# Converting the second block's weights piece by piece, every 0.8 units of matmul work

## The chip, the cores and the metric

The kernel runs on one core of a Trainium2 chip. The metric is the device time of one execution in microseconds. An execution uses TensorE for matmuls (PE, with its weight loads PEld), VectorE (DVE), ScalarE (ACT), GpSimd (POOL) and SyncE (SP), whose queue issues all of this kernel's DMAs in order.

## The reference

Three stages follow each other on 4 sequences of 576 tokens and 512 features. First an attention with 8 heads of 64: a windowed one over the three nearest neighbours on either side, plus one over tokens that are averaged by fours. Then two blocks with residuals:

```python
def _moe_ref(x, g_ln, w_ch1, w_ch2):                        # w_ch1 512 x 2048
    xn = (x - mean(x)) / np.sqrt(var(x) + 1e-06) * g_ln
    return x + np.maximum(xn @ w_ch1, 0.0) @ w_ch2
...
def _moe2_ref(x, w_tok1, w_tok2, w_ch1, w_ch2):             # w_ch1 512 x 1536
    h = np.maximum(x.transpose(0, 2, 1) @ w_tok1, 0.0) @ w_tok2
    u = x + h.transpose(0, 2, 1)
    return u + np.maximum(u @ w_ch1, 0.0) @ w_ch2
```

The inputs q, k and v are float32, all weights are float64.

## The kernel before

**Tiling.** The 2304 tokens are cut into 9 chunks of 256. A *unit* is 128 hidden columns of a block's first weight matrix with the same 128 rows of its second: 16 units for the first block, 12 for the second. For a chunk and a unit, `g1` (line 622) multiplies the chunk's turned activations with the first matrix (12 matmuls, 128x256, into an `h` tile). ACT applies the ReLU and DVE forms the remainder (lines 635, 636, tile `ht`). `g2` (line 641) multiplies that with the second matrix (6 matmuls, 128x512, into `acc` tiles). Products are made of two parts each, a high and a low one, in three passes: high x high, high x low, low x high. The sequence has 9 x 16 units of the first block and 9 x 12 of the second, 252 in all. Units 0 to 143 are the first block's, and unit 144 is the second block's first one. In the emission `g1` of a unit stands ahead of `g2` of the unit before it.

**Weights.** The weights are float64, so each has to be taken apart. A unit comes in two *pieces* of 512 KB: piece 0 is its first matrix, piece 1 its second. `load_unit` (DMA at line 190) brings a piece into a staging tile `st`; two of them exist in the part of the program that matters here. `convert_steps` (line 143) turns it into the high and low parts in five steps: three on DVE (lines 149, 154, 159, tile `cv`), one on ACT (line 164, the high part), one on DVE (line 167, the low part). `split_unit` pins the place of the first of them among the other pinned work. After the five steps of a piece, `w_split` (line 817) emits the load of the next one. The load's own wait is that the third step (line 159) has read the staging tile. The 12 units of the second block, once converted, stay in SBUF for all nine chunks.

**Beside it.** The token mixing of the second block needs, for each of the 4 sequences, five loads `xr` (lines 705 and 707), their split on ACT and POOL (lines 713, 714, tile `xs`), the matmuls of `tok1` (line 729, tile `k`), a ReLU (lines 738, 739) and, for each chunk, those of `tok2` (line 760, tile `g`). A chunk's activations are turned by DVE in 32x32 blocks (line 579, tile `xc`) and then by 32 small DMAs of 16 KB per chunk (line 586, tile `xt`). These, the weight pieces and the `xr` loads all go through SP's one queue.

**What sets the order.** `put(pos, f)` (line 775) hangs work on a position that is counted in units: at a whole number ahead of `g2` of that unit, at a half behind it. Behind that a scheduler with a model of the engines' times sets each engine's final order; pinned instructions keep theirs.

Of the kernel before, what the change touches and what calls it, by code (L numbers as in the profile page):

```python
# [91 lines left out]
def block_kernel(ctx: ExitStack, tc: tile.TileContext, qk, vw, vg, g_ln, wa, t1, t2, wb, band, out):  # L92
    nc = tc.nc
    UA = wa.shape[0]
    UB = wb.shape[0]
# [80 lines left out]
    NPC = 2 * DM // QW  # L176
# [598 lines left out]
    def put(pos, f, *args):  # L775
        u, half = divmod(int(2 * pos), 2)
        u = min(u, NSEQ - 1)
        (bg if half else mid)[u].append(lambda: f(*args))
# [32 lines left out]
    def w_load(n):  # L811
        while n and nl[0] < len(pieces) and nl[0] - nsp[0] < sp["n"]:
            load_unit(*pieces[nl[0]])
            nl[0] += 1
            n -= 1
# [128 lines left out]
    bw = base[NCH - 1]  # L944
    put(bw + 1, units_b)
    put(bw + 1, lambda: w_load(sp["n"]))
    for m in range(UB):
        put(bw + 3.5 + m, w_split, NPC)
    for c in range(NCH, 2 * NCH):
        put_prep2(c, base[c] - 1)  # L950
    put_tok(2, base[NCH + 2])
# [96 lines left out]
```

## Time and profile before

| | |
|---|---|
| median of 3 runs | 951.56 us (948.16 to 956.02) |
| profiled execution, its own time | 952.27 us |
| its span | 950.5 us |
| PE busy | 916.2 us, 96% |
| DVE busy | 447.9 us, 47% |
| ACT busy | 280.6 us, 30% |
| POOL busy | 147.5 us, 16% |
| loads of second-block weights | 24 of 512 KB |

Busy time is what the profiler saw an engine execute; matmuls overlap in the array, so their single durations (some 0.28 and 0.40 us) are longer than the distance at which they follow each other. A timeline row gives the start in us from the span's start, the time it covers, the engine, the line and the operation, and in brackets how long the engine was idle ahead of it and for whom it waited.

### The profile page before, as it was taken

Reading aid. Unit: us, or ns where it says so; the run is one execution under the profiler, and the core shown is the slowest. Engines: PE = TensorE matmul, PEld = TensorE weight load, DVE = VectorE, ACT = ScalarE, POOL = GpSimd, SP = SyncE. Lnnn points to the kernel's source line nnn. Section 1 sums busy time; section 2 is a strip of 40 time slices with the busy share of each in tenths; the row PEclk is TensorE's granted clock in tenths of the full one; section 3 lists DMA queues with packets and bytes.
Section 4 is the critical chain, followed back from the end, with each engine's and each line's share of the span. In section 5 each row is a group of like instructions: output and inputs, shape, how many; then the busy total and the mean of one; then the engine's idle time right before and its main releaser. Section 6 shows DMA issues by size and latency. Waiting matters only on the chain.

```text
span 950.5 us, 17304 instructions
## 1 busy us (share of the span) xinstructions
PE 916.2 (96%) x6702; PEld 801.0 (84%) x6702; DVE 447.9 (47%) x1044; ACT 280.6 (30%) x809; POOL 147.5 (16%) x176
## 2 busy tenths in 40 slices
PE   7879999899999999999999999999999999999998
PEld 5667878778888888888889988787888888999997
DVE  4785788794225252276312267896322322222211
ACT  5444344344443343323111122332112111111111
POOL 6443214213322221111010000111001000000000
PEclk9888999999999999999999999999999999999999
DMA  8653565534232132234212025663212211110100
GB/s 221 183 188 115 157 194 182 169 104 106 83 105 67 47 104 62 67 106 144 73 28 63 23 83 150 190 187 111 57 44 63 51 36 33 45 35 13 44 23 23
DMA packets 113121, 89.78 MB, mean 94 GB/s; under 512 B 73264, under 2 KB 91952, under 8 KB 113040
## 3 DMA queue, kind: packets, MB, share of 16 engines
q1 hardware_dynamic: 113040, 88.68, 32.7%
q8 instruction: 53, 0.87, 0.4%
q14 instruction: 28, 0.23, 0.1%
HBM read 66.62 MB, written 14.16 MB: 85 GB/s over the span
## 4 chain that ended last, share of the span: by engine, by line
PE 78%; DVE 8%; DMA 8%; SPq 2%; ACT 1%; issue 1%; POOL 1%; DVEq 0%; ACTq 0%
PE h L629 33%; PE acc L650 31%; DMA up_scr<-od 2%; DMA st<-in_wb_dram 2%; PE k L650 2%; PE k L729 2%; SPq L586 2%; DMA xr<-x_scr 2%; DVE cv L159 2%; PE g L760 2%; DVE cv L154 1%; PE g L282 1%; PE g L363 1%; PE g L318 1%; PE g L468 1%
## 5 line engine op out<-in xcount | busy, mean ns | idle before, releaser
L629 PEld LDWEIGHTS h<-xt,w 128*128 128x128 f32 x3024 | 395.5, 190 | 25.0 <-ACT w L164 1.9
L629 PE MATMUL h<-xt,w 128*128 128x256 f32 x3024 | 411.8, 284 | 1.6 <-ACT w L164 1.0
L650 PE MATMUL acc<-w,ht 128*128 128x512 f32 x1416 | 378.7, 399 | 8.1 <-ACT ht L635 3.6
L650 PEld LDWEIGHTS acc<-w,ht 128*128 128x128 f32 x1416 | 252.2, 189 | 61.5 <-ACT ht L635 5.7
L636 DVE SCALAR_TENSOR_TENSOR ht<-h,ht 128x256 fp32r<-128x256 f32 x252 | 105.8, 421 | 354.6 <-ACT ht L635 354.3
L635 ACT ACTIVATE ht<-h 128x256 fp32r<-128x256 f32 x252 | 96.4, 383 | 394.0 <-PE h L629 370.4
L714 POOL TENSOR_TENSOR xs<-xr,xs 128x512 fp32r<-128x512 f32 x20 | 26.6, 1330 | 292.4 <-ACT xs L713 292.4
L164 ACT ACTIVATE w<-cv 128x512 fp32r<-128x512 f32 x56 | 35.5, 635 | 70.7 <-DVE cv L159 70.5
L346 POOL TENSOR_TENSOR vg<-vg 72x256 f32<-72x256 f32 x39 | 32.8, 841 | 144.7 <-DMA vg<-in_vg_dram 143.5
L167 DVE TENSOR_TENSOR w<-cv,w 128x512 fp32r<-128x512 f32 x56 | 42.6, 764 | 6.4 <-ACT w L164 6.2
L159 DVE SCALAR_TENSOR_TENSOR cv<-st,cv 128x512 int32<-128x512 int32 (+4 forms) x63 | 42.8, 684 | 0.6
L154 DVE SCALAR_TENSOR_TENSOR cv<-st,cv 128x512 int32<-128x512 int32 (+4 forms) x63 | 42.4, 677 | 0.7
L515 POOL TENSOR_TENSOR x<-x,pt 128x256 f32<-128x256 f32 (+2 forms) x44 | 28.0, 649 | 80.2 <-DMA x<-up_scr 47.9
L729 PE MATMUL k<-xs,t1w 128*128 128x512 f32 (+1 forms) x120 | 33.5, 410 | 2.2 <-ACT xs L713 1.4
L760 PE MATMUL g<-r,t2w 128*128 128x512 f32 x120 | 34.0, 395 | 0.0
L593 ACT ACTIVATE xt<-xt 128x512 fp32r<-128x512 f32 x30 | 19.0, 632 | 50.0 <-DMA xt<-xc 49.9
L149 DVE TENSOR_SCALAR cv<-st 128x512 int32<-128x512 int32 (+4 forms) x63 | 25.8, 412 | 13.8 <-DMA st<-in_wb_dram 8.9
L594 DVE TENSOR_TENSOR xt<-xt 128x512 fp32r<-128x512 f32 x30 | 20.6, 686 | 23.6 <-ACT xt L593 23.5
L650 PE MATMUL k<-w,ht 128*128 128x512 f32 x96 | 27.6, 409 | 0.1
L729 PEld LDWEIGHTS k<-xs,t1w 128*128 128x128 f32 (+1 forms) x120 | 19.1, 188 | 7.2 <-ACT xs L713 2.1
L502 ACT ACTIVATE pt<-g,rz 128x64 f32<-128x64 f32 (+1 forms) x78 | 17.4, 322 | 23.2 <-DVE rz L492 21.8
L760 PEld LDWEIGHTS g<-r,t2w 128*128 128x128 f32 x120 | 20.9, 189 | 3.0
(160 smaller groups left out, 700.6 us busy)
## 6 DMA issues: line engine op xcount, KB each, us to landing
st<-in_wa_dram SPq DMA_DIRECT2D x28, 512.0 KB
st<-in_wb_dram SPq DMA_DIRECT2D x24, 512.0 KB
xt<-xc SPq DMA_DIRECT2D x480, 16.0 KB
qk<-in_qk_dram SPq DMA_DIRECT2D x13, 579.0 KB
x_scr<-x SPq DMA_DIRECT2D x18, 256.0 KB
x<-x_scr SPq DMA_DIRECT2D x9, 512.0 KB
out_dram<-x SPq DMA_DIRECT2D x18, 256.0 KB
vw<-in_vw_dram SPq DMA_DIRECT2D x13, 319.9 KB
```

Of the source, the lines that this page charges most:

```text
L154: nc.vector.scalar_tensor_tensor(out=f, in0=h, scalar=-0x40000000, in1=f, op0=ALU.bitwise_and, op1=ALU.bitwise_or)
L159: nc.vector.scalar_tensor_tensor(out=f, in0=l, scalar=29, in1=f, op0=ALU.logical_shift_right, op1=ALU.bitwise_or)
L164: nc.scalar.activation(out=hi, in_=f.bitcast(F32), func=ACTF.Copy)
L167: nc.vector.tensor_tensor(out=lo, in0=f.bitcast(F32), in1=f32(hi), op=ALU.subtract)
L346: nc.gpsimd.tensor_tensor(out=vd[:, :, :, :D], in0=vd[:, :, :, :D], in1=vgt[:, :, o:o + 128].rearrange("p c (h d) -> p c h d", h=2), op=AL ...
L515: (eng or nc.gpsimd).tensor_tensor(out=x, in0=x, in1=tmp[rows, tl:tl + k].rearrange("p t h d -> p t (h d)"), op=ALU.add)
L629: nc.tensor.matmul(out=hp[:, :CN], lhsT=w[:, 0, a, kk * 128:(kk + 1) * 128], rhs=xT[c][:, kk, e, :], start=(n == 0), stop=(n == 3 * KD - 1),)
L635: nc.scalar.activation(out=t[:, 0], in_=hp[:, :CN], func=ACTF.Relu)
L636: nc.vector.scalar_tensor_tensor(out=t[:, 1], in0=hp[:, :CN], scalar=0.0, in1=f32(t[:, 0]), op0=ALU.max, op1=ALU.subtract)
L650: nc.tensor.matmul(out=acc[c, j], lhsT=t[:, a, j * 128:(j + 1) * 128], rhs=w[:, 1, e, :], start=(m == 0 and n == 0), stop=(last and n == 2),)
L729: nc.tensor.matmul(out=rps[b, m], lhsT=tokw["t1"][rows, a, n, m * 128:(m + 1) * 128], rhs=t[rows, e, :], start=(n == 0 and i == 0), stop=( ...
L760: nc.tensor.matmul(out=ps, lhsT=tokw["t2"][:, a, m, o:o + 128], rhs=r_t[b][:, m, e, :], start=(i == 0), stop=(i == len(ops) - 1),)
```

## The change

Before, the 12 units' conversions hang on positions 131.5, 132.5, ..., 142.5, two pieces each (`bw` is 128). After, the 24 pieces hang on 131, 131.8, ..., 149.4, one each. The number of instructions on DVE, on POOL and of DMAs is unchanged.

```diff
--- before.py
+++ after.py
@@ -944,8 +944,8 @@
     bw = base[NCH - 1]
     put(bw + 1, units_b)
     put(bw + 1, lambda: w_load(sp["n"]))
-    for m in range(UB):
-        put(bw + 3.5 + m, w_split, NPC)
+    for m in range(UB * NPC):
+        put(bw + 3 + 0.8 * m, w_split, 1)
     for c in range(NCH, 2 * NCH):
         put_prep2(c, base[c] - 1)
     put_tok(2, base[NCH + 2])
```

How the order moves is seen at three places. The first is SP's queue from the sixth load of a weight piece (piece 5, the first row) on. The rows `xt<-xc` are the small turn DMAs of the second block's first chunk. Before:

```order
L190 DMA st<-in_wb_dram 128x1024
L586 DMA xt<-xc 32x4x32 x3
L190 DMA st<-in_wb_dram 128x1024
L586 DMA xt<-xc 32x4x32 x6
L190 DMA st<-in_wb_dram 128x1024
L586 DMA xt<-xc 32x4x32 x10
L707 DMA xr<-x_scr_110 128x512
L190 DMA st<-in_wb_dram 128x1024 x2
```

After:

```order
L190 DMA st<-in_wb_dram 128x1024
L586 DMA xt<-xc 32x4x32 x19
L707 DMA xr<-x_scr_110 128x512
L190 DMA st<-in_wb_dram 128x1024 x2
L705 DMA xr<-x_scr_108 64x512 x2
L190 DMA st<-in_wb_dram 128x1024 x2
```

Pieces 6 and 7 stood inside the turn DMAs and now stand behind them and behind the token load; where pieces 8 and 9 followed that load, pieces 6 and 7 do.

The second place is DVE between the remainders (line 636) of units 138 and 142. L149, L154, L159 and L167 are the steps of a conversion. Before:

```order
L636 SCALAR_TENSOR_TENSOR ht<-h,ht 128x256
L159 SCALAR_TENSOR_TENSOR cv<-st,cv 128x512
L167 TENSOR_TENSOR w<-cv,w 128x512
L765 TENSOR_TENSOR x<-g,x 128x512
L167 TENSOR_TENSOR w<-cv,w 128x512
L579 STREAM_TRANSPOSE xc<-x 128x512
L765 TENSOR_TENSOR x<-g,x 128x512
L149 TENSOR_SCALAR cv<-st 128x512
L154 SCALAR_TENSOR_TENSOR cv<-st,cv 128x512
L636 SCALAR_TENSOR_TENSOR ht<-h,ht 128x256
L159 SCALAR_TENSOR_TENSOR cv<-st,cv 128x512
L167 TENSOR_TENSOR w<-cv,w 128x512
```

After:

```order
L636 SCALAR_TENSOR_TENSOR ht<-h,ht 128x256
L765 TENSOR_TENSOR x<-g,x 128x512
L579 STREAM_TRANSPOSE xc<-x 128x512
L636 SCALAR_TENSOR_TENSOR ht<-h,ht 128x256
L765 TENSOR_TENSOR x<-g,x 128x512
L636 SCALAR_TENSOR_TENSOR ht<-h,ht 128x256
L594 TENSOR_TENSOR xt<-xt 128x4x128
L579 STREAM_TRANSPOSE xc<-x 128x512
L149 TENSOR_SCALAR cv<-st 128x512
L154 SCALAR_TENSOR_TENSOR cv<-st,cv 128x512
L636 SCALAR_TENSOR_TENSOR ht<-h,ht 128x256
L159 SCALAR_TENSOR_TENSOR cv<-st,cv 128x512
```

Before, the conversions of pieces 6 and 7 stand here; after, three units pass with none, and the L149 behind them is that of piece 6.

The third place is PE around the last unit of the second block's first chunk, B11 in its first use (the `acc` row of six is its second-matrix group, which needs the last piece). Before:

```order
L629 MATMUL h<-xt,w 128x256 x2
L650 MATMUL acc<-w,ht 128x512 x4
L629 MATMUL h<-xt,w 128x256 x10
L650 MATMUL acc<-w,ht 128x512 x2
L629 MATMUL h<-xt,w 128x256 x12
L729 MATMUL k<-xs,t1w 128x512 x6
L650 MATMUL acc<-w,ht 128x512 x6
```

After:

```order
L629 MATMUL h<-xt,w 128x256 x2
L650 MATMUL acc<-w,ht 128x512 x2
L629 MATMUL h<-xt,w 128x256 x22
L760 MATMUL g<-r,t2w 128x512 x8
L729 MATMUL k<-xs,t1w 128x512
L760 MATMUL g<-r,t2w 128x512 x4
L729 MATMUL k<-xs,t1w 128x512 x5
L650 MATMUL acc<-w,ht 128x512 x6
```

Token work of the next batches (12 matmuls of line 760, 6 of line 729) now stands ahead of that group. From the first-matrix group of unit 134 up to it stand 276 matmuls of 128x256 and 240 of 128x512 before, and 276 and 258 after.

## Rows read from the trace of the kernel before

**Rows 1.** The page: span, busy time of two engines, PE's granted clock by slices.
```profile
span 950.5 us, 17304 instructions
...
PE 916.2 (96%) x6702; PEld 801.0 (84%) x6702; DVE 447.9 (47%) x1044; ACT 280.6 (30%) x809; POOL 147.5 (16%) x176
...
PEclk9888999999999999999999999999999999999999
```

**Rows 2.** Chain of waits, undisturbed stretch: start us, us, engine, tile, line, count.
```profile
506.88 1.43 PE h L629 x12
508.31 1.39 PE acc L650 x6
```

**Rows 3.** PE's timeline, unit 134 to the last group.
```profile
560.26 1.59 PE L629 MATMUL h<-xt,w 128*128 128x256 f32 x12
...
602.36 1.20 PE L650 MATMUL acc<-w,ht 128*128 128x512 f32 x4 [0.80 <-ACT ht L635]
603.80 0.74 PE L650 MATMUL acc<-w,ht 128*128 128x512 f32 x2 [0.25 <-DVE ht L636]
...
629.73 0.73 PE L650 MATMUL acc<-w,ht 128*128 128x512 f32 x2 [0.45 <-DVE ht L636]
...
646.46 0.73 PE L729 MATMUL k<-xs,t1w 128*128 128x512 f32 x2 [1.38 <-ACT xs L713]
647.91 1.19 PE L729 MATMUL k<-xs,t1w 128*128 128x512 f32 x4 [0.72 <-POOL xs L714]
...
654.51 1.65 PE L650 MATMUL acc<-w,ht 128*128 128x512 f32 x6
...
943.44 2.91 PE L650 MATMUL acc<-w,ht 128*128 128x512 f32 x12
```

**Rows 4.** DVE's groups, 557 to 654: count, busy us, mean ns, idle before.
```profile
L167 DVE TENSOR_TENSOR w<-cv,w 128x512 fp32r<-128x512 f32 x24 | 18.3, 763 | 4.0 <-ACT w L164 3.9
L159 DVE SCALAR_TENSOR_TENSOR cv<-st,cv 128x512 int32<-128x512 int32 x24 | 18.0, 750 | 0.2
L154 DVE SCALAR_TENSOR_TENSOR cv<-st,cv 128x512 int32<-128x512 int32 x24 | 17.0, 709 | 0.2
L149 DVE TENSOR_SCALAR cv<-st 128x512 int32<-128x512 int32 x24 | 11.2, 467 | 9.0 <-DMA st<-in_wb_dram 8.9
```

**Rows 5.** DVE's timeline: first steps of pieces 1, 6, 8, 16, 19, 23; last step.
```profile
562.46 0.42 DVE L149 TENSOR_SCALAR cv<-st 128x512 int32<-128x512 int32 x1
...
578.59 0.43 DVE L149 TENSOR_SCALAR cv<-st 128x512 int32<-128x512 int32 x1
...
592.12 1.03 DVE L149 TENSOR_SCALAR cv<-st 128x512 int32<-128x512 int32 x1 [2.28 <-DMA st<-in_wb_dram]
...
621.38 0.43 DVE L149 TENSOR_SCALAR cv<-st 128x512 int32<-128x512 int32 x1
...
635.10 0.41 DVE L149 TENSOR_SCALAR cv<-st 128x512 int32<-128x512 int32 x1
...
649.72 0.42 DVE L149 TENSOR_SCALAR cv<-st 128x512 int32<-128x512 int32 x1
...
652.49 1.24 DVE L167 TENSOR_TENSOR w<-cv,w 128x512 fp32r<-128x512 f32 x1 [0.70 <-ACT w L164]
```

**Rows 6.** SP's timeline: load 5, turn DMAs, the token load, loads 8 and 9.
```profile
571.91 0.33 SPq L190 DMA_DIRECT2D st<-in_wb_dram  x1
572.29 1.87 SPq L586 DMA_DIRECT2D xt<-xc  x3
...
580.02 7.20 SPq L586 DMA_DIRECT2D xt<-xc  x10
587.32 0.53 SPq L707 DMA_DIRECT2D xr<-x_scr  x1
587.97 0.83 SPq L190 DMA_DIRECT2D st<-in_wb_dram  x2
```

## The prediction, made before the result was known

> **What bounds the kernel now.** First the page's busy shares: PE is busy 96% of the 950.5 us span, DVE 47%, and the granted clock is in its top tenth from the fifth slice on [rows 1]. So PE is the bound, and a change that leaves PE's work alone can only touch the few us in which PE waits. Next the chain of waits in an undisturbed stretch gives PE's pace: twelve 128x256 matmuls in 1.43 us (0.119 each) and six 128x512 in 1.39 us (0.232 each) [rows 2]. With that pace I priced the part that the change can reach. I number the units of the second block B0 to B11 and its pieces 0 to 23; piece 2k holds the first matrix of Bk, piece 2k+1 its second. PE's timeline starts the first-matrix group of unit 134 (ten units ahead of B0) at 560.26 and the second-matrix group of B11 in its first use at 654.51 [rows 3]: 94.25 us. In PE's order 276 matmuls of the first kind and 240 of the second stand between: 276 x 0.119 + 240 x 0.232 = 88.5 us. So PE loses **5.8 us** there, and the timeline names most of the places: 0.80 and 0.25 us near 603, 0.45 at 629.7, 1.38 and 0.72 at 646 to 648 [rows 3]; the rest lies in matmuls that start late without a named wait. Behind 656 PE runs without a gap to its last group at 943.44 [rows 3].
>
> Why PE loses time there is seen on DVE. Its 24 conversions cost 0.47 + 0.71 + 0.75 + 0.76 us a piece [rows 4], the last of them ends at 653.7 [rows 5], and DVE is idle in front of the first step 9.0 us for loads and in front of the last step 4.0 us for ACT [rows 4]. The row of first steps shows the pace: piece 8 starts at 592.12, piece 23 at 649.72, 15 intervals of **3.84 us** [rows 5]. That is the cycle of two staging buffers: a load is issued when the third step has read a buffer (587.97), lands 4.15 us later (592.12) [rows 5, 6], and DVE needs some 2 us, with other work between, to free it. PE takes 2.82 us of unit work per unit plus fill, so two pieces per unit at 3.84 us would be far too slow; the pieces hold only because they start ten units ahead.
>
> **The change part by part.** It adds and removes nothing: 24 loads, 24 conversions, DVE 1045 instructions in either order, POOL's order the same. It moves.
>
> 1. *Pieces 6 and 7 fall behind a turn on SP.* Before, load 5 goes out at 571.91, then come three 16 KB turn issues (1.87 us), load 6, six issues, load 7, ten issues (7.20 us), a token load and loads 8 and 9 at 587.97 [rows 6]. After, load 5 is followed by 19 issues, the token load, and only then loads 6 and 7. The transposes that feed the 19 stand as far ahead on DVE as before, so nothing holds them: at 0.65 us each (between the 0.62 of the three and the 0.72 of the ten) they take 12.4 us from 572.3. SP reaches the token load at 584.7 and load 6 at 585.3, by the 0.65 us between those two before [rows 6]. With the same 4.15 us landing piece 6 starts at **589.4**: two pieces behind the order of before, but 2.7 us earlier than piece 8 did. SP is not delayed elsewhere: its issues are the same in number.
>
> 2. *The last 18 pieces.* From there 17 intervals stand to piece 23. Unknown is the pace. Bounds from the rows: the fastest stretch is pieces 1 to 6, 562.46 to 578.59, five intervals of 3.23 us; the slowest is pieces 16 to 19, 621.38 to 635.10, three of 4.57 us [rows 5]; the last four (635.10 to 649.72) take 3.66 each. The buffers, the loads and the DVE steps are the same, so I take **3.8**, between the whole stretch and its end: piece 23 starts at 589.4 + 17 x 3.8 = 654.0, that is 4.3 us later than before.
>
> 3. *PE has more to do meanwhile.* In the new order 258 instead of 240 of the larger matmuls stand between the two marks: token work of the next batch (12 of line 760, 6 of line 729) was drawn ahead of B11. That is 18 x 0.232 = **4.2 us** of work that PE does while it would wait, and has not to do later.
>
> 4. *Sum.* Before, B11's second group started 654.51 - 649.72 = 4.8 us after piece 23's first step [rows 3, 5] (last subtraction at 652.49, then the unit's own activation). After: 654.0 + 4.8 = 658.8. Taking off the 4.2 us already done gives 654.6, against 654.5: **+0.1 us**. A token activation pair (two steps of line 739) now stands inside piece 23's conversion; 0.7 us of ACT's step runs beside it, so I put it at nothing; without that cover it costs 1.3 us. The earlier stalls of PE (603, 630, 646) are inside this sum: all that counts is when the last piece is ready. If no piece came late at all, PE would reach B11's second group at 560.26 + 276 x 0.119 + 258 x 0.232 = 653.0 with the 4.2 us done, which is the 5.8 us again: no gain beyond that. Behind it the two orders give each unit the same lead (a unit's first group stands at least one whole unit ahead of its second), so nothing follows.
>
> The profiled execution took 952.27 us (span 950.5), 0.7 above the median of 951.56. The sum is against the profiled one; on the median it gives **951.7 us**.
>
> *A rule against a row.* The load of 512 KB lands 4.15 us after its issue here [rows 5, 6]. The Trainium skill, page "DMA: Bandwidth & Descriptors", section "Anatomy of one DMA", gives a fixed part of about 2.0 us plus bytes over 436 GB/s; an estimate from that page is 3.2 us. It is a fit for loads issued by GpSimd, and these are SP's; the row is the longer by a quarter. By the page's figure the pace would be nearer 3.4 and the sum nearer rival A; I go by the row.
>
> **The rivals.** *A. The conversions leave PE's path.* With one piece at a time on DVE its buffer comes free sooner, the next load goes out sooner, and the pace is 3.23 to 3.6. Then piece 23 starts at 644.3 to 650.6, PE waits little or not at all, and the gain is 3.3 us to the full 5.8: 945.8 to 948.4. For it: the fastest stretch was at 3.23 [rows 5]. Against it: that stretch is the first, where DVE and SP had the least other work between the pieces. The page's estimate for a load would give this case, the landing row doesn't. Chance 0.20.
>
> *B. A hold on SP that PE can't cover (slower).* Loads 18 to 23 alternate with token loads of the next batch, each of which waits until POOL has split the one before. If these set the beat, pieces come every 4.57 us as 16 to 19 did. PE's drawn-in work covers 3.8; each 0.1 us above it costs 1.7 us. At 4.1 it is +5.2, at 4.35 +9.5, at 4.57 over all 17 intervals +13.2 (964.8). PE would then stand before B8 to B11, and the activations of those units, queued on ACT and DVE behind the waiting conversions, would be late as well. For it: the row of 4.57, and 646.46, where PE waited for such a token split. Against it: the long stretch averaged 3.84 with the same token loads in it. Chance 0.10 from 4.1 on, half of it beyond 4.35.
>
> *C. The order changes and nothing on the chip follows*, because the two buffers and not the emission set the pace and the drawn-in work just refills the gap: that is my forecast, with pace 3.6 to 4.1 and -3.3 to +5.2 us. Chance 0.70.
>
> **Numbers.** A measurement of this kernel can tell about 1% (9.5 us). A gain of that size is excluded by the 5.8 us that PE loses, so faster has 0.02, for what the runs scatter. Slower than that needs rival B beyond 4.35: 0.05. The rest, 0.93, is within 1%. The range takes C whole and most of A: 946.3 (5.4 less) to 957.0 (5.3 more); left out are the last of A and B from 4.1 on, with what the runs scatter by themselves (948.16 to 956.02).
>
> **What would show it.** In the changed trace: loads 6 and 7 right behind a token load near 585; piece 6's first step near 589 and piece 23's near 654; B11's second group near 659; between the two marks PE's idle time near 5 to 6 us, now late in the stretch, before B9 to B11, not at 603. Right behind it PE without gaps to the end. Wrong would be: piece 23 before 650 (A) or after 659 (B), or PE gaps behind 665, which I exclude.

## The result, and the profile after

The changed kernel takes **959.27 us** (median of 11 runs, 951.43 to 963.41), the kernel before 952.1 (11 runs beside it): ratio **1.0075** [1.0052, 1.0097]. The forecast was 951.7, with a range up to 957.0. The change is within 1%, as forecast, but slower by more than the runs scatter. The profiled execution took 959.72 us, a span of 957.9, 7.4 above the profiled one of before [rows 1]. The same page lines of the changed kernel:

```profile
span 957.9 us, 17313 instructions
...
PE 921.4 (96%) x6702; PEld 803.4 (84%) x6702; DVE 446.8 (47%) x1044; ACT 281.2 (29%) x809; POOL 146.2 (15%) x176
...
PEclk9789999999999999999999999998999999999999
```

The work is the same, PE's busy time is 5.2 us longer, and the clock row has a new 8 far behind the start. SP's timeline after (start us, us, issues) answers to [rows 6]:

```profile
570.94 0.33 SPq L190 DMA_DIRECT2D st<-in_wb_dram  x1
571.32 13.24 SPq L586 DMA_DIRECT2D xt<-xc  x19
584.65 0.53 SPq L707 DMA_DIRECT2D xr<-x_scr  x1
585.29 0.85 SPq L190 DMA_DIRECT2D st<-in_wb_dram  x2
...
641.65 3.67 SPq L190 DMA_DIRECT2D st<-in_wb_dram  x2
645.42 1.14 SPq L705 DMA_DIRECT2D xr<-x_scr  x2
650.39 0.33 SPq L190 DMA_DIRECT2D st<-in_wb_dram  x1
```

Loads 6 and 7 go out at 585.29 behind 19 turn DMAs (forecast 585.3). The last rows show SP's one queue near the end: the second load of the pair at 641.65 has to wait for its staging buffer, the pair spans 3.67 us, and the two token loads stand behind it. DVE's first steps of pieces 6, 21, 22 and 23 and the last low part (compare [rows 5]):

```profile
589.02 0.99 DVE L149 TENSOR_SCALAR cv<-st 128x512 int32<-128x512 int32 x1 [1.07 <-DMA st<-in_wb_dram]
...
646.27 0.42 DVE L149 TENSOR_SCALAR cv<-st 128x512 int32<-128x512 int32 x1
649.34 0.43 DVE L149 TENSOR_SCALAR cv<-st 128x512 int32<-128x512 int32 x1 [1.91 <-DMA st<-in_wb_dram]
...
654.11 0.41 DVE L149 TENSOR_SCALAR cv<-st 128x512 int32<-128x512 int32 x1
...
658.64 0.69 DVE L167 TENSOR_TENSOR w<-cv,w 128x512 fp32r<-128x512 f32 x1 [0.70 <-ACT w L164]
```

Piece 23 starts at 654.11. The next view is PE's timeline (in brackets its idle time and for whom it waited) from unit 134 to the last group; it answers to [rows 3]:

```profile
559.38 1.59 PE L629 MATMUL h<-xt,w 128*128 128x256 f32 x12
...
637.00 0.73 PE L729 MATMUL k<-xs,t1w 128*128 128x512 f32 x2 [1.56 <-ACT xs L713]
638.66 1.20 PE L729 MATMUL k<-xs,t1w 128*128 128x512 f32 x4 [0.93 <-POOL xs L714]
...
644.47 1.20 PE L729 MATMUL k<-xs,t1w 128*128 128x512 f32 x4 [0.88 <-POOL xs L714]
...
650.73 0.70 PE L729 MATMUL k<-xs,t1w 64*128 64x512 f32 x2 [2.24 <-ACT xs L713]
651.52 1.22 PE L650 MATMUL acc<-w,ht 128*128 128x512 f32 x2
...
656.12 3.50 PE L629 MATMUL h<-xt,w 128*128 128x256 f32 x22
659.45 2.03 PE L760 MATMUL g<-r,t2w 128*128 128x512 f32 x8
...
662.48 1.32 PE L729 MATMUL k<-xs,t1w 128*128 128x512 f32 x5
663.64 1.55 PE L650 MATMUL acc<-w,ht 128*128 128x512 f32 x6
...
949.74 2.91 PE L650 MATMUL acc<-w,ht 128*128 128x512 f32 x12
```

Between the marks lie 104.26 us for 276 x 0.119 + 258 x 0.232 = 92.7 us of work: PE loses **11.6 us** where it lost 5.8. The named waits sum to 6.4 us (0.42, 0.18, 1.56, 0.93, 0.17, 0.88, 2.24, not all shown) against 3.6 before; all but the first are for token splits. What has grown besides is the loss to the granted clock, which was 1.00 in all this stretch in the profiled execution of before. By stretches of 2 us (stretch, its length, PE busy, weight loads, DVE, ACT, POOL, then the granted clock, DMA share, GB/s):

```profile
648.00:650.00 2.00, 0.49 (x5) 0.28 (x3) 0.66 (x2) 0.00 (x0) 0.00 (x0) 1.00 0.43 105
650.00:652.00 2.00, 1.18 (x3) 0.68 (x4) 1.97 (x3) 1.42 (x3) 1.25 (x1) 0.71 0.34 53
652.00:654.00 2.00, 2.00 (x7) 0.70 (x7) 2.00 (x4) 0.70 (x2) 0.10 (x1) 0.50 0.69 236
654.00:656.00 2.00, 2.00 (x6) 1.71 (x7) 1.96 (x5) 1.61 (x3) 0.00 (x0) 0.50 0.31 113
656.00:658.00 2.00, 2.00 (x11) 1.90 (x11) 1.94 (x2) 0.06 (x2) 1.28 (x1) 0.58 0.00 0
658.00:660.00 2.00, 2.00 (x17) 1.91 (x16) 0.69 (x1) 0.90 (x3) 0.00 (x0) 1.00 0.39 131
```

PE waits 2.24 us to 650.7, and behind it the clock stands at 0.50, the lower level of 1.2 GHz, until about 657.7. It costs 0.58 + 1.00 + 1.00 + 0.84 = 3.4 us of full-speed work. In the stretches at 0.50 PE is shown as fully busy: the loss is visible in the clock column and in long matmuls alone.

The books close on 7.4: 0.9 us won ahead of the marks, 5.8 more lost between them (4.2 us of work moved in), 1.4 behind (949.74 - 663.64 = 286.1, where 288.9 - 4.2 = 284.7 was due) and 1.1 in the tail, behind PE's last group.

The same split holds without a profile. Every run lists its span and its mean clock; span x (1 - clock) is what the clock took, the rest is the time at full clock. Means over 11 runs after and 25 before (those beside e13 to e16 below; the runs of it beside the other experiments give 11.9 to 13.0 and 936.6 to 937.9): clock 15.2 against 12.5 us, the rest 941.8 against 937.4. So some 4.4 us are waiting and some 2.7 the clock, with a standard error of 1.0. The kernel before is not free of falls: its mean clock goes from 0.983 to 0.991 over these runs.

### The profile page after: what moved, and what is told of

Its sections match the earlier page's. It is cut to its first block, busy times and chain, and to the rows that moved or that the text cites. A ratio compares the mean times of both kernels' runs of the same rounds, so it can differ in the third digit from the quotient of the medians.

```text
span 957.9 us, 17313 instructions
## 1 busy us (share of the span) xinstructions
PE 921.4 (96%) x6702; PEld 803.4 (84%) x6702; DVE 446.8 (47%) x1044; ACT 281.2 (29%) x809; POOL 146.2 (15%) x176
## 4 chain that ended last, share of the span: by engine, by line
PE 81%; DVE 8%; DMA 7%; ACT 1%; SPq 1%; issue 1%; POOL 0%; DVEq 0%; ACTq 0%
PE h L629 34%; PE acc L650 32%; DMA st<-in_wb_dram 2%; PE k L729 2%; PE g L760 2%; DMA up_scr<-od 2%; PE k L650 2%; DVE cv L159 1%; DVE cv L154 1%; PE g L282 1%; DVE w L167 1%; PE g L363 1%; PE g L468 1%; PE g L407 1%; PE g L318 1%
## 5 line engine op out<-in xcount | busy, mean ns | idle before, releaser
L346 POOL TENSOR_TENSOR vg<-vg 72x256 f32<-72x256 f32 x39 | 30.5, 781 | 145.6 <-DMA vg<-in_vg_dram 122.7
L159 DVE SCALAR_TENSOR_TENSOR cv<-st,cv 128x512 int32<-128x512 int32 (+4 forms) x63 | 46.0, 735 | 0.5
L167 DVE TENSOR_TENSOR w<-cv,w 128x512 fp32r<-128x512 f32 x56 | 40.7, 729 | 4.9 <-ACT w L164 4.7
L154 DVE SCALAR_TENSOR_TENSOR cv<-st,cv 128x512 int32<-128x512 int32 (+4 forms) x63 | 41.8, 668 | 0.7
L729 PE MATMUL k<-xs,t1w 128*128 128x512 f32 (+1 forms) x120 | 36.1, 428 | 6.0 <-ACT xs L713 4.1
L149 DVE TENSOR_SCALAR cv<-st 128x512 int32<-128x512 int32 (+4 forms) x63 | 26.0, 416 | 19.1 <-DMA st<-in_wb_dram 12.2
```

The lines of the kernel that those rows point to most:

```text
L154: nc.vector.scalar_tensor_tensor(out=f, in0=h, scalar=-0x40000000, in1=f, op0=ALU.bitwise_and, op1=ALU.bitwise_or)
L159: nc.vector.scalar_tensor_tensor(out=f, in0=l, scalar=29, in1=f, op0=ALU.logical_shift_right, op1=ALU.bitwise_or)
L167: nc.vector.tensor_tensor(out=lo, in0=f.bitcast(F32), in1=f32(hi), op=ALU.subtract)
L346: nc.gpsimd.tensor_tensor(out=vd[:, :, :, :D], in0=vd[:, :, :, :D], in1=vgt[:, :, o:o + 128].rearrange("p c (h d) -> p c h d", h=2), op=AL ...
L729: nc.tensor.matmul(out=rps[b, m], lhsT=tokw["t1"][rows, a, n, m * 128:(m + 1) * 128], rhs=t[rows, e, :], start=(n == 0 and i == 0), stop=( ...
```

## The experiments

All ratios are to the kernel before on the same chip, with their 95% intervals. Two theories stood first. T: token loads that alternate with pieces 18 to 23 on SP hold PE. W: the last pieces themselves come late. The first four kernels:

**e1**, piece by piece with the start and the mean pace of before.

```diff
-    for m in range(UB * NPC):
-        put(bw + 3 + 0.8 * m, w_split, 1)
+    for m in range(UB * NPC):
+        put(bw + 3.5 + 0.5 * m, w_split, 1)
```

> One part of the change alone: one piece at a time, but at the old pace and start (131.5 to 143, every 0.5 units). Theory T (token order): what costs the time is that token matmuls of the third sequence were drawn ahead of units B8 to B11 and wait on PE for token loads that alternate on SP with the loads of the last pieces; here they do so too (behind pieces 17, 18 and 19), so 955 to 960 us and PE idle of 4 to 6 us around 635 to 655 in front of line 729. Theory W (late weights): the slower pace of 0.8 units brings the last pieces late; here the pace is the old one, so 950 to 953 us.

Measured 954.79, 1.0029 [1.0003, 1.0055]: less than half of the loss, and between the two forecasts.

**e2**, two pieces every 1.6 units.

```diff
-        put(bw + 3 + 0.8 * m, w_split, 1)
+    for m in range(UB):
+        put(bw + 3 + 1.6 * m, w_split, NPC)
```

> The other part alone: unit by unit as before, but every 1.6 units from 131, the mean pace of the change. Theory W (late weights): 957 to 961 us, as the change. Theory T (token order): it depends on where the token matmuls fall; they are drawn in earlier here (third sequence's first loads behind pieces 8 and 10), so their loads meet fewer pieces at the end: 952 to 957 us.

Measured 956.16, 1.0057 [1.0035, 1.0078]: most of the loss, though nothing is emitted piece by piece. The time lies in T's range, 0.8 us short of W's; e1 and e2 do not decide between the two.

**e3**, the token loads on GpSimd's queue (changed kernel).

```diff
 def xs_load(b, n):
...
-            nc.sync.dma_start(
+            nc.gpsimd.dma_start(
```

> The changed kernel with the token loads (lines 705, 707) issued by GpSimd in place of SP, so that they no longer stand between the pieces' loads; the scheduler then also draws the token matmuls to other places. Theory T: the waits of line 729 go away, the last piece's first step comes at 645 to 650 in place of 654, PE idles under 3 us from 630 to 655, the granted clock stays up: 946 to 952 us. Theory W: the pieces are late all the same: 956 to 960 us.

Measured 960.6, 1.0099 [1.0074, 1.0124]. T as the only cause falls: the token loads are off SP, PE has no wait for a token split near the end any more, and the time is longer. Piece 23 starts at 658.23 there, and PE waits for units' activations instead, 3.31 us in one place.

**e4**, the token matmuls of the third sequence held until B11's second group.

```diff
+            with (tc.issue_after(mark[0]) if b == 2 else nullcontext()):
                 nc.tensor.matmul(
                     out=rps[b, m], ...
```

> The changed kernel with the token matmuls of the third and fourth sequence kept behind B11's second group on PE (an order edge, no wait). PE then has 36 matmuls of 128x512 (8.3 us) less to do while the weights come, and pieces 19 to 23 are loaded back to back. Theory T: PE waits for weights only and the last piece comes some 5 us sooner; with less work drawn ahead the end moves little: 953 to 958 us, no wait of line 729. Theory W: the last piece comes as late as in the change and the 8.3 us are missing as cover: 964 to 968 us.

Measured 961.6, 1.0108 [1.008, 1.0135]. That is 3.6 us above T's range and 2.4 below W's, so neither was right about the size; without a wait of line 729 the time is longer, not shorter. Without token work in between, PE's waits for pieces merge. Its timeline (lines 636 and 651 of this kernel are lines 635 and 650 of the others):

```profile
636.16 3.10 PE L651 MATMUL acc<-w,ht 128*128 128x512 f32 x6 [3.00 <-ACT ht L636]
...
643.43 2.93 PE L651 MATMUL acc<-w,ht 128*128 128x512 f32 x6 [0.53 <-ACT ht L636]
```

ACT's timeline shows what that unit's activation (the last row) stood behind:

```profile
635.20 0.63 ACT L164 ACTIVATE w<-cv 128x512 fp32r<-128x512 f32 x1 [3.75 <-DVE cv L159]
635.74 0.37 ACT L636 ACTIVATE ht<-h 128x256 fp32r<-128x256 f32 x1
```

It is queued behind a conversion's high part, for which ACT waited 3.75 us. The group of six behind PE's wait of 3.00 us takes 3.10 us where it takes 1.55: the clock stands at 0.50 from 635, still inside the wait, to about 648.7. Of its excess of 10.0 us over the runs of the kernel before beside it, the clock takes 18.5 - 11.9 = 6.6 us in the mean of its four runs, the larger part.

**e5 and e6**, the changed kernel and the kernel before without their last two pieces.

```diff
-        pieces.extend((UA + i, part) for i in range(UB) for part in range(NPC))
+        pieces.extend((UA + i, part) for i in range(UB - 1) for part in range(NPC))
...
-        return wt[m if c < NCH else UA + m]
+        return wt[m if c < NCH else UA + min(m, UB - 2)]
```

> The changed kernel without pieces 22 and 23: B11 uses B10's matrices, so its result is another and its matmuls are as many. Theory L (the last pieces come late, PE waits for them and for token splits whose loads stand behind them on SP, and the granted clock falls to half behind the longest wait): piece 21, last now, starts as in the changed kernel near 646 us, PE's wait of 2.24 us near 650 and the 3.4 us at half clock are gone, the token waits of 637 to 645 stay. Time 952 to 954.5, ratio 1.000 to 1.003. Rival D (the loss lies in token work that stands in front of PE, not in the last pieces): time stays at 957 or more, ratio over 1.005.

> The kernel before without pieces 22 and 23, as in e5. Theory L: PE already waits little for the last two pieces (the named waits, 2.1 us at 646 to 648, are for token splits), so it gains 0 to 2.5 us: 949 to 951.6, ratio 0.9975 to 1.000, and e5 stands closer to it than the changed kernel stands to the kernel before. Rival D: the same gain here, but the distance to e5 stays at 7 us.

Measured 0.9989 [0.9968, 1.0009] and 1.0004 [0.9981, 1.0027]. Taking the same two pieces away is worth 8 us in the changed kernel and nothing in the kernel before: the loss hangs on the last two pieces. (e5's forecast was 952 to 954.5; it came out at 950.99.) The earlier token waits stay in e5:

```profile
634.14 0.73 PE L729 MATMUL k<-xs,t1w 128*128 128x512 f32 x2 [1.83 <-ACT xs L713]
635.49 1.20 PE L729 MATMUL k<-xs,t1w 128*128 128x512 f32 x4 [0.62 <-POOL xs L714]
...
646.68 0.98 PE L729 MATMUL k<-xs,t1w 64*128 64x512 f32 x6
```

The last row is the group that waited 2.24 us at 650.73: it does not wait here, its token load no longer stands behind the last pieces, and the clock stays at 1.00 through this stretch.

**e7 and e8**, the price of a wait by itself: a chain of copies on GpSimd holds PE at unit 216, where nothing is converted (6 copies, then 12).

```diff
+        for k in range(6):
+            nc.gpsimd.tensor_copy(idle, f32(t[:, 0]) if k == 0 else idle)
+        ins = nc.tensor.matmul(out=psg("g")[:, :CN], lhsT=ident, rhs=idle, start=True, stop=True)
```

> The kernel before with one added wait of PE far from any conversion: at unit 216 a chain of 6 copies (128x256) on GpSimd feeds one added matmul, and PE's later work is held behind that. Theory L with its clock part: a wait of about 2 us costs itself, or itself and up to 3 us more at half clock, by whether the granted clock falls behind it. Without a clock part: it costs itself and no more.

> As e7 with 12 copies, a wait of about 4 us. With the clock part: the granted clock falls to half behind it for several us, and the time grows by the wait and 2 to 4 us more. Without: by the wait alone, and the granted clock stays at 1.00.

Measured 1.0045 [1.0027, 1.0064] and 1.0068 [1.0045, 1.0092]. The held matmul in e7:

```profile
844.90 0.70 PE L962 MATMUL g<-idle,ident 128*128 128x256 f32 x2 [1.85 <-POOL idle L961]
845.25 1.75 PE L760 MATMUL g<-r,t2w 128*128 128x512 f32 x6
```

and in e8:

```profile
852.53 1.22 PE L962 MATMUL g<-idle,ident 128*128 128x256 f32 x2 [4.62 <-POOL idle L961]
853.19 2.90 PE L760 MATMUL g<-r,t2w 128*128 128x512 f32 x6
```

with the granted clock of e8 there:

```profile
850.00:852.00 2.00, 0.00 (x0) 0.00 (x0) 0.00 (x0) 0.00 (x0) 1.75 (x5) 1.00 0.18 28
852.00:854.00 2.00, 1.47 (x4) 1.20 (x5) 0.00 (x0) 0.08 (x1) 0.42 (x2) 0.57 0.13 20
854.00:856.00 2.00, 2.00 (x7) 1.57 (x6) 0.69 (x1) 0.55 (x1) 0.00 (x0) 0.57 0.00 0
856.00:858.00 2.00, 2.00 (x16) 1.91 (x15) 1.43 (x3) 0.38 (x1) 0.00 (x0) 1.00 0.00 0
```

The wait of 4.62 us is followed by six matmuls in 2.74 us instead of 1.39 and costs 0.86 + 0.86 = 1.7 us more by the clock; wait, clock and small gaps sum to 6.5 us, and 0.68% of 951 is 6.5. The wait of 1.85 us leaves the clock at 1.00, in this execution; of the 4.3 us that e7 costs (2.6 to 6.1), its trace shows that wait and two later gaps of 0.85 and 0.3 us, 3.0 in all. The Trainium skill, page "TensorE: Matmul & The Clock Gate", section "Part 1: The HAM clock gate (the "warmup" mystery)", says that an idle PE is put to half its clock and takes a stretch of work to get it back; e8 agrees (0.57 behind the wait, 1.00 from 856 on), and so in kind does the changed kernel, behind shorter waits.

A narrower form of W came next: what decides is how many of loads 6 and 7 stand behind the turn on SP (two in the changed kernel and e2, one in e1, none before).

**e9**, unit by unit at one unit's distance as before, but half a unit earlier; **e10**, piece by piece every 0.65 units.

```diff
-        put(bw + 3.5 + m, w_split, NPC)
+        put(bw + 3 + m, w_split, NPC)
```
```diff
-        put(bw + 3 + 0.8 * m, w_split, 1)
+        put(bw + 3 + 0.65 * m, w_split, 1)
```

> Unit by unit at one unit's distance as before, but from 131 instead of 131.5 on. In this order loads 6 and 7 go out inside the turn, as before the change. Theory L in its narrower form (what decides is how many of loads 6 and 7 stand behind the turn's DMAs on SP; two of them in the changed kernel, none before): no change, ratio 0.998 to 1.002. If the earlier start itself did harm, over 1.003.

> Piece by piece as in the change, but every 0.65 units instead of 0.8. In this order load 6 goes out inside the turn and load 7 behind the last 16 of its DMAs: one piece is held, not two. Theory L, narrower form: between the two kernels, as e1 was, ratio 1.001 to 1.005. If emission piece by piece did the harm by itself: as the change, over 1.006.

Measured 0.9976 [0.9954, 0.9998] and 1.0070 [1.0047, 1.0094]. e9 is slightly faster than both kernels. e10 has one piece behind the turn and is as slow as the change with two: the count is not what decides. Its piece 23 is as late as the changed kernel's (table).

**e11 and e12**, the turn DMAs of the second block's first chunk on GpSimd's queue, in the changed kernel and in the one before.

```diff
-                nc.sync.dma_start(
+                (nc.gpsimd if c == NCH else nc.sync).dma_start(
```

> The changed kernel with the 32 turn DMAs of the second block's first chunk on GpSimd's queue instead of SP's; nothing stands between loads 5 and 12 on SP. Theory L: the pieces come at the buffers' pace without the 12 us pause, the last ones some 4 us or more earlier, PE stops waiting for them and the clock doesn't fall: ratio below 1.002, at best 0.995. If GpSimd issues so slowly that the chunk's turned activations come late, PE waits for those instead and the time stays above 1.005.

> The kernel before with the same move. Theory L: it loses the named waits for conversions (about 1.5 us near 603 and 630), the last pieces come earlier too, ratio 0.994 to 1.000, and it is within 0.2% of e11, since the slip that told the two apart is gone.

Measured 1.0111 [1.0067, 1.0154] and 1.0069 [1.004, 1.0098]: both missed. In e11 the pieces run without a pause up to the eleventh (594.17). DVE's timeline from there:

```profile
610.51 0.43 DVE L636 SCALAR_TENSOR_TENSOR ht<-h,ht 128x256 fp32r<-128x256 f32 x1 [5.35 <-ACT ht L635]
614.23 0.69 DVE L594 TENSOR_TENSOR xt<-xt 128x512 fp32r<-128x512 f32 x1 [3.29 <-ACT xt L593]
...
616.04 0.42 DVE L149 TENSOR_SCALAR cv<-st 128x512 int32<-128x512 int32 x1
```

The twelfth piece now stands behind other work that DVE waits for, and on SP the next loads stand behind 20 turn DMAs of the second chunk (606.68 to 620.92). The pause moved from one turn to the next and grew: piece 23 starts at 662.18. That lateness and time go together is seen once more; that the time falls when the first turn is off SP is not. In both, PE also waits for the chunk's turned activations (0.70 us at 600.37 in e11, 1.42 us at 599.19 in e12), so they are no clean test.

**e13 to e16** take what was left apart: the emission of before, unit by unit every unit, with the start alone moved (131.5 before).

```diff
-        put(bw + 3.5 + m, w_split, NPC)
+        put(bw + 2 + m, w_split, NPC)
```

That is e13; e14 has 2.5, e15 has 4 and e16 has 5.

> Unit by unit every unit as before, from 130 instead of 131.5. In this order loads up to 9 go out ahead of the token load behind the turn, two more than before. Account 1 (the last pieces' lateness decides): piece 23 starts 4 us or more earlier against PE, PE's waits for pieces go, ratio 0.993 to 0.998. Account 2: 1.000. If the loads now delay the turn's DMAs, PE waits for the chunk's turned activations near 600 and the ratio is over 1.002.

> The same from 130.5. Account 1: as e13, ratio 0.993 to 0.999. Account 2: 1.000.

> The same from 132: loads 6 and 7 stand behind the turn's 19 DMAs as in the changed kernel, but the emission is unit by unit. Account 1: piece 23 near 92 to 94 us behind the remainder of unit 134 (87 before, 92 in the changed kernel), ratio 1.004 to 1.009. Emission piece by piece as the cause by itself: 1.000.

> The same from 133: loads 4 to 7 stand behind the turn, four pieces where the changed kernel has two. Account 1: piece 23 about 7 us later still, ratio 1.010 to 1.018. The slip of pieces 6 and 7 alone as the cause: as e15.

Measured 1.0012 [0.9992, 1.0032], 0.9975 [0.9957, 0.9992], 1.0056 [1.0036, 1.0076] and 1.0143 [1.0122, 1.0165]. All kernels by the start of piece 23's first step, counted from the remainder (line 636) of unit 110, which lies ahead of all that the edits move (491.86 before, 490.99 in the changed kernel):

| kernel | emission | piece 23 | ratio |
|---|---|---|---|
| e14 | unit, from 130.5 | 154.0 | 0.9975 |
| e13 | unit, from 130 | 156.2 | 1.0012 |
| e9 | unit, from 131 | 157.4 | 0.9976 |
| before | unit, from 131.5 | 157.9 | 1 |
| e4 | change, token matmuls held | 159.8 | 1.0108 |
| e1 | pieces, 131.5, every 0.5 | 161.9 | 1.0029 |
| the change | pieces, 131, every 0.8 | 163.1 | 1.0075 |
| e10 | pieces, 131, every 0.65 | 164.2 | 1.0070 |
| e2 | unit, 131, every 1.6 | 164.5 | 1.0057 |
| e15 | unit, from 132 | 164.9 | 1.0056 |
| e12 | before, turn moved | 167.1 | 1.0069 |
| e3 | change, token loads moved | 169.2 | 1.0099 |
| e16 | unit, from 133 | 169.6 | 1.0143 |
| e11 | change, turn moved | 170.2 | 1.0111 |

Up to about 158 us the lateness costs nothing that shows. From 162 on all kernels are slower, whether units or pieces are emitted; e15, which has the emission of before and the lateness of the change, has three quarters of its loss. The order within 163 to 170 is not strict: what PE has to do meanwhile differs, and the lateness is that of one execution each. In e7 and e8, whose order is that of the kernel before up to about 770 us, it is 158.3 and 159.6. e4 is the one row off the line, and it is the one that took PE's work out of the stretch. e13 missed its forecast: its pieces are earlier, yet PE waits 2.19 us at 631.93 for a unit's activation and 1.82 us at 651.70 for a token split. Being early has no more to give, since other waits are then last.

In e2 and e15, whose pieces are about as late as the change's, PE's longest wait is the same one as in the change: it is for the split of the two 64-row token loads. The first row is e2's, the second e15's:

```profile
643.00 0.80 PE L729 MATMUL k<-xs,t1w 64*128 64x512 f32 x2 [2.96 <-ACT xs L713]
643.21 0.79 PE L729 MATMUL k<-xs,t1w 64*128 64x512 f32 x2 [3.46 <-ACT xs L713]
```

Behind both the clock is at 0.50 to about 649. In the kernel before, e9 and e14 PE has no named wait for that split.

PE in e16, the latest unit-by-unit kernel:

```profile
653.30 1.04 PE L650 MATMUL acc<-w,ht 128*128 128x512 f32 x2 [2.60 <-ACT ht L635]
654.75 1.22 PE L650 MATMUL acc<-w,ht 128*128 128x512 f32 x2 [0.40 <-DVE w L167]
```

It waits for a unit's activation, which stands on ACT behind a token split, which waited 4.71 us for its load; then for a low part; and it runs at half clock (1.22 us for two matmuls). The clock loss of e16 is 18.3 us in the mean, 5.8 above before, and its time at full clock 8.0 above.

## Why the prediction was wrong, step by step

**Step 1 was right, its last digit by luck.** Load 6 was forecast for 585.3 and piece 6 for 589.4; they came at 585.29 and 589.02. The turn DMAs began 1.0 us earlier than forecast (571.32) and took 0.8 longer (13.24 against 12.4), and the two errors cancel.

**Step 2 was right.** Forecast 17 intervals of 3.8 us and piece 23 at 654.0; the trace has (654.11 - 589.02) / 17 = 3.83 and 654.11. Since PE ran 0.9 us earlier there, the piece is 5.3 us later against PE (163.12 against 157.86), not 4.3. Rival A's pace didn't come.

**Step 3 failed.** The 18 drawn-in matmuls were to be work "that PE does while it would wait". Their place in PE's order is behind the 22 first-matrix matmuls of B11 and of the unit after it, at 659.45 to 663.64. The last low part ends at 659.33: when PE reached them, the weights were there. Only the activations of those two units were still to come:

```profile
659.71 0.66 ACT L635 ACTIVATE ht<-h 128x256 fp32r<-128x256 f32 x2 [1.10 <-PE h L629]
```

So the 18 hid about 1 us at most (an estimate: from 659.45 to the end of the activations at 660.37), not 4.2. PE had waited earlier, from 637 to 651, in front of work that stands ahead of them. The 4.2 us were done in advance and are indeed saved later (284.7 was due behind the mark), but they gave back next to nothing of the lateness. Work covers a wait only if it stands ahead of the instruction that waits.

**Step 4 failed with it, in two terms.** First, the sum took one event, the last piece, as the only thing that counts and called the earlier stalls part of it. B11's second group started 9.5 us behind piece 23's first step, not 4.8. The named waits near the end were for token splits, and the pieces made them late: DVE's third step of piece 20, from 643.20 to 644.96, frees the buffer; the second load of the pair and the token loads behind it (645.42) go out on SP only then; their split waits for them on ACT until 650.04, and PE goes on at 650.73.

```profile
650.04 0.63 ACT L713 ACTIVATE xs<-xr 128x512 fp32r<-128x512 f32 x1 [4.41 <-DMA xr<-x_scr]
```

e5 shows that it is the last pieces that make them matter: without pieces 22 and 23 the last of these waits is gone, and with it the whole loss. Second, the clock was not in the sum at all. [Rows 1] shows no fall behind the start, and I read that as a property of the stretch; it was one of the profiled execution. In e7, whose order here is that of the kernel before, the same four matmuls as in [rows 3] (1.19 us there) ran for the most part at half clock:

```profile
644.73 1.77 PE L729 MATMUL k<-xs,t1w 128*128 128x512 f32 x4 [0.70 <-POOL xs L714]
```

e8 prices it: 1.7 us behind one wait of 4.62. In the change it is 3.4 us in the profiled execution and 2.7 in the mean. Besides, the sum put the token activation pair inside piece 23's conversion at nothing. From its first step to the end of its low part that conversion took 5.22 us (654.11 to 659.33) where it took 4.01 before, and the pair's two steps on DVE (654.56 and 655.76, 0.6 us each) stand between its first three; the trace names no wait of PE for it.

**Rival B** named the alternation on SP, the activations behind conversions and the right sign, but asked for a pace of 4.1 or more. The pace was 3.83 and the loss came all the same, so its condition was wrong. **Rival C**, the forecast, went up to +5.2 us; the ratio makes it +7.1, with +4.9 to +9.2 as its interval. The size is outside by little, but what C said, that the drawn-in work just refills the gap, is not what the trace shows. "PE gaps behind 665, which I exclude" is right to within small gaps: 1.4 us in all.

Open: how the 4.4 us of waiting divide between the pieces themselves and the token splits behind them. e3 and e4 took the token side away and changed the rest too much to tell. Whether a given wait of some 2 us brings the clock down is not settled either: it did in the change (2.24) and did not in e1 (2.20 us at 656.69, clock 1.00 throughout 650 to 660) or in e6, where PE waits 2.05 us at 652.75 for the same 64-row split.

## What to carry to other kernels

When work is said to hide a wait, find its place in the engine's order: it must stand ahead of the instruction that waits. Where a chain of loads arrives just ahead of its use, as in the kernel before, a delay of 5 us has a price of its own and cannot be set off against work that stands behind. And a wait of TensorE of a few us should be priced with the clock that may fall behind it: here from a third of the wait (e8) to more than the rest of the excess (e4).

## What the runs showed of the hardware

The granted clock stood at 0.50 over work that is shown as 100% busy: 651 to 657.7 in the change, behind waits of 0.88 and 2.24 us with about 4 us of work between them, 852 to 856 in e8 around the end of 4.62 us, and 635 to 648.7 in e4 from inside a wait of 3.00 us on, with more waits at half speed. DVE's third conversion step, 0.68 us as a rule, took 1.76 us while GpSimd ran a token split beside it:

```profile
643.20 1.76 DVE L159 SCALAR_TENSOR_TENSOR cv<-st,cv 128x512 int32<-128x512 int32 x1
```

and the split, from the changed kernel's GpSimd timeline:

```profile
642.88 1.54 POOL L714 TENSOR_TENSOR xs<-xr,xs 128x512 fp32r<-128x512 f32 x1 [4.28 <-ACT xs L713]
```

The three other third steps that began inside a split took 1.45 to 1.65 us; where the split began second, at 637.02, the step took 0.69 us and the split 1.58 instead of about 1.3. The forecast put conversions and splits side by side at no cost. A turn DMA of 16 KB issued by GpSimd took about 0.6 us (9 in 5.37 us in e11), much as on SP.
